# A retention-attention and two-MoE kernel: two column orders of the first MoE layer are interleaved

## The chip, the cores and the metric

The kernel runs on one core of one Trainium2 chip. The metric is the device time of one execution in microseconds (us). A core has a matrix engine (PE), a vector engine (DVE), a scalar engine (ACT), GpSimd (POOL) and a queue engine (SP) that issues transfers. Each works off its own list of instructions in a fixed order and waits for the others by semaphores. A kernel is timed over several executions; one more is recorded by the profiler, and all durations below are from that one.

## The reference

```python
# attention with decay: 2 batches, 8 heads, 768 tokens, head size 64, blocks of 64
out[:, :, sl] = (q k^T * Dmask) v + (q * lam_pow) kv_state     # kv_state runs over the blocks
# first MoE layer, dense: x is [1536, 512], w_in [512, 2048], w_out [2048, 512]
h = x @ w_in
g = h * np.clip(h + 3.0, 0.0, 6.0) / 6.0
x = g @ w_out
# second MoE layer: 8 experts, 192 tokens each
logits = x @ w_gate                      # every token goes to an expert with room, best logit first
out[mask] = np.maximum(x[mask] @ w1[e], 0.0) @ w2[e]
```

## The kernel before, in words

The 1536 tokens are 12 chunks of 128; chunks 0 to 5 are the first batch, 6 to 11 the second. Every matrix product that has to be exact is made from 16-bit pairs (a high and a low half), so one product is three matmuls (`mm3`, L221 to L223).

**Attention** of chunk c: scores S (L452), their masked copy sm on DVE (L458), the state product kv (L467) with its DVE step sbd, and the output xo (L494, L498). The two halves of xo leave through ACT (L504) and DVE (L505) as xT, the 16-bit pair that is the x of the first layer.

**The first layer** is 52 units of h, each one PSUM buffer of 512 columns for 12 matmul groups: group 0 is 8 units of chunks 0 to 3 one at a time (`h0_u`, the first four column blocks of w_in), group 1 is 12 units over chunks 0 to 3 together (`h1_u`, column blocks 4 to 15), group 2 is 8 units of chunks 4 and 5, group 3 is 8 units of chunks 6 and 7, group 4 is 16 units of chunks 8 to 11. A unit leaves by four instructions: r on ACT (L535) and DVE (L536), then the pair g by ACT (L406) and DVE (L416). h has three PSUM buffers.

**Weights.** w_in and w_out arrive as 64-bit numbers in eight parts each (`wis`, `wos`) and are turned into 16-bit pairs by a chain that changes engines: ACT L383 (L381 on DVE for the first three parts of w_in), POOL L385, then DVE L387, L389, L391, then ACT L406 and DVE L416. The part in work is called `wid` or `wod`. Each part of w_out is also transposed by DMA (`wt`, in the pool H of two buffers, which wid, wod and the logits' halves use too) and multiplied by the gate's weights (`wp`, L585 and L586), which gives the weights of the logits.

**Logits, routing, experts.** lq (L610) are the logits of four chunks each, lg (L625) sums them up. Then come seven routing phases (mp on PE, POOL L775, DVE L800 and L809, ACT L803), in which PE fills its time with x2p, the product g w_out (L647: 48 matmuls of 512 columns for each of chunks 0 to 7, of 384 columns for 8 to 11; their last 128 columns are x2q and x2t). After routing, rk and pos give each token its place, and POOL scatters the tokens by 24 indirect DMAs, 12 of `xsa` and 12 of `xsb` (L877). A transposing DMA brings each pair of experts its rows (`xs`, L897, L898), and the experts' products are hp (L922) and po (L952).

**What sets the order.** The program is not written in the order in which it runs. Each step is handed to a planner (`Plan`) with its engine, an estimated cost, what it depends on, its buffers and a key. The planner walks through an imagined time; of the steps that could start on an engine within a small window it takes the one with the smallest key. What comes out is one fixed list for each engine. A dependency that is given to the planner alone moves a step in these lists; at run time an instruction waits only for data, for a buffer, or for those ahead of it on its engine. `unit_key` is the key of each unit in a running count over the list `order`; `w0_key` is the key of the first part of w_out.

Of the kernel before, what the change touches and what calls it, by code (L numbers as in the profile page):

```python
# [16 lines left out]
NCH = 12  # L17
# [31 lines left out]
class Plan:  # L49
# [122 lines left out]
def c_se(n):  # L172
    return 0.1 + n * 0.00083
# [19 lines left out]
def fused_kernel(ctx, tc, raw_d, lam_d, win_d, wout_d, wg_d, w1_d, w2_d, out):  # L193
# [229 lines left out]

    RAW_KEY = [0, 0, 2, 2.5, 3.5, 6.5, 16, 17, 18, 19, 20, 21]

# [85 lines left out]
    h_mm = {}  # L511
    win = {}

    def h_unit(g, u, key, lo_eng):
# [11 lines left out]
        def mms():  # L526
            for f in range(nf):
# [6 lines left out]
        r = buf("Q", [P, nf, T], F32, f"r{g}_{u}")  # L534
        t = add("se", c_se(nf * T), lambda: se.activation(r[:], ps[:], AF.Relu, bias=c3, scale=2.0 ** -31), [t], [ps, r], key)  # L535
        t = add("ve", c_ve(nf * T), lambda: ve.scalar_tensor_tensor(r[:], r[:], 6.0 * 2.0 ** -11, ps[:], op0=OP.min, op1=OP.mult),  # L536
                [t], [ps, r], key)
        for c in cs:
            g_done.setdefault(c, []).extend(
                split(lambda: r[:], lambda: (gt[:, 0, fo:fo + nf, to:to + T], gt[:, 1, fo:fo + nf, to:to + T]), nf * T, 1.0, lo_eng, [t], [r, gt], key + 1)  # L540
                if c == c0 else g_done[c0][-1:])
# [9 lines left out]
    t = 20.0  # L551
    order = [(g, u) for g in range(5) for u in range(len(UNITS[g]))]
    for i, (g, u) in enumerate(order):
# [3 lines left out]
    for c in range(NCH):  # L557
        attention(c, max(0.5 + 4 * c, unit_key[GOF[c], 0] - 40) if c > 3 else 7 * c)
        if c == 0:
            weights(win_d, win, 1024.0, "wi", lambda k: 10 + 7 * k, lambda k: "ve",  # L560
                    lambda k: [0, 1, 3, 3, 6, 6, 7, 7][k], pre=win_ld)
    for g, u in order:
        h_unit(g, u, unit_key[g, u], "ve")

    warm_last.deps = [h_mm[order[10]]]

# [5 lines left out]
    t_pj = []  # L572
    w0_key = unit_key[4, 0] - 16

    def project(k, t, dst):
# [6 lines left out]
        def pj():  # L582
# [6 lines left out]
    weights(wout_d, wout, 2048.0, "wo", lambda k: w0_key + 7 * k, lambda k: "ve", lambda k: 30 + k, project,  # L589
            lambda k: [out_done[[4, 4, 6, 6, 8, 8, 10, 10][k]]])  # L590
    w1t = C([P, 16, NE], F32, "wpt")
# [450 lines left out]
```

## Time and profile before

| | |
|---|---|
| three timed runs | 512.02, 514.68, 515.46 us; median 514.68 |
| the profiled execution | 515.91 us; 514.0 us from its first to its last instruction |
| TensorE clock over the span | 0.986 of full speed |
| PE busy | 485.0 us, 94% |
| DVE busy | 397.8 us, 77% |
| ACT busy | 309.0 us, 60% |
| POOL busy | 166.6 us, 32% |

Busy shares are averages over stages with different limits. Up to about 50 us loads, conversions and the first attention chunks share the time; from 50 to 205 us runs the first layer with the rest of attention; from 215 to 345 us the routing phases; then scatter and the experts. A matmul's end is modelled, so a short wait on PE can be hidden in the row ahead of it; starts are the safer numbers.

### The profile page before, as it was taken

To read this page: it belongs to the slowest core of one execution; us is meant where nothing else is said; L and a number is where in the kernel's file an instruction comes from. 1 tells how busy PE (TensorE), PEld (TensorE's weight loads), DVE (VectorE), ACT (ScalarE), POOL (GpSimd) and SP (SyncE) were. 2 spreads that over 40 slices of the span, in tenths; PEclk is the share of its full clock that TensorE was granted. 3 is DMA by queue.
4 is the path that set the end of the run, shared out by engine and by line. 5 is a ranking of instruction groups with operands and counts; after the bars stand their busy time and mean duration, and the time that the engine had idled before them with its cause. 6 is when DMAs were issued, how large, how long until landed. Compare 5 with 4: busy or idle time off the path is not lost.

```text
span 514.0 us, 10307 instructions
## 1 busy us (share of the span) xinstructions
PE 485.0 (94%) x4241; PEld 296.7 (58%) x4243; DVE 397.8 (77%) x707; ACT 309.0 (60%) x486; POOL 166.6 (32%) x174
## 2 busy tenths in 40 slices
PE   7687998999999999999999999999969999999995
PEld 3476444688785444534434443556459676776762
DVE  7689999988688877589899889877524878889620
ACT  1476959764556664377669558745423767687510
POOL 2013343120222220167347436618860312223211
PEclk9889999999999999999999999999979999999999
DMA  7999326220264550000000000667368999995011
GB/s 224 400 416 412 148 83 246 84 42 2 83 246 91 97 94 8 2 1 1 1 1 2 1 1 7 240 246 240 132 149 261 327 400 356 360 354 215 1 42 41
DMA packets 44910, 77.86 MB, mean 151 GB/s; under 512 B 33080, under 2 KB 34112, under 8 KB 38720
## 3 DMA queue, kind: packets, MB, share of 16 engines
q1 hardware_dynamic: 42752, 70.82, 41.0%
q0 software_dynamic: 2112, 6.39, 3.3%
q8 instruction: 33, 0.54, 0.4%
q14 instruction: 13, 0.11, 0.1%
HBM read 63.46 MB, written 6.40 MB: 136 GB/s over the span
## 4 chain that ended last, share of the span: by engine, by line
DVE 38%; issue 22%; PE 18%; POOL 8%; ACT 8%; DMA 5%; POOLq 0%; SPq 0%; DVEq 0%; ACTq 0%
PE x2p L647 9%; DVE G L809 7%; DVE r L536 4%; DVE G L800 3%; DVE g L416 3%; POOL w L410 3%; POOL out L877 2%; ACT kd L439 2%; DVE sm L458 2%; ACT g L406 2%; DVE eq L782 2%; PE h L221 2%; DVE wid L391 2%; PE cp L828 2%; PE h L223 2%
## 5 line engine op out<-in xcount | busy, mean ns | idle before, releaser
L647 PE MATMUL x2p<-wo,g 128*128 128x512 f16 (+1 forms) x576 | 124.6, 362 | 0.0
L221 PE MATMUL h<-xT,wi 128*128 128x256 f16 (+2 forms) x304 | 90.8, 306 | 2.8 <-DVE r L536 2.8
L222 PE MATMUL h<-xT,wi 128*128 128x256 f16 (+2 forms) x304 | 90.7, 306 | 0.0
L223 PE MATMUL h<-xT,wi 128*128 128x256 f16 (+2 forms) x304 | 90.6, 306 | 0.0
L647 PEld LDWEIGHTS <-g 128*128 128x128 f16 x576 | 52.5, 99 | 55.6 <-issue 10.5
L775 POOL TENSOR_SCALAR eq<-mrow,m 128x128 bf16<-128x128 f32 x56 | 56.7, 1030 | 84.6 <-DVE on L748 52.1
L416 DVE SCALAR_TENSOR_TENSOR w<-ws,w 128x1024 f16<-128x1024 f32 x58 | 71.4, 1276 | 5.8 <-ACT w L406 5.8
L922 PE MATMUL hp<-xs,w 128*128 128x192 f16 x768 | 67.4, 251 | 3.8 <-DMA xs<-xsa 3.8
L922 PEld LDWEIGHTS <-w 128*128 128x128 f16 x768 | 65.1, 100 | 7.6 <-issue 5.2
L952 PE MATMUL po<-w,h 128*64 128x512 f16 (+1 forms) x384 | 64.1, 380 | 0.1
L406 ACT ACTIVATE w<-ws 128x1024 f16<-128x1024 f32 x64 | 63.9, 1048 | 0.1
L809 DVE TENSOR_SCALAR G<-mrow,m 128x1408 bf16<-128x1408 f32 (+10 forms) x77 | 52.0, 706 | 0.0
L385 POOL TENSOR_SCALAR wod<-wod 128x1024 f32<-128x1024 f32 x8 | 22.5, 2818 | 89.3 <-ACT wod L383 75.5
L406 ACT ACTIVATE g<-r 128x512 f16<-128x512 f32 (+1 forms) x52 | 30.8, 595 | 30.5 <-DVE r L536 29.6
L952 PEld LDWEIGHTS <-h 128*64 128x64 f16 (+1 forms) x384 | 29.0, 104 | 31.8 <-issue 1.7
L416 DVE SCALAR_TENSOR_TENSOR g<-r,g 128x512 f16<-128x512 f32 (+1 forms) x52 | 34.3, 662 | 11.4 <-ACT g L406 11.0
L536 DVE SCALAR_TENSOR_TENSOR r<-r,h 128x512 f32<-128x512 f32 (+1 forms) x52 | 33.1, 639 | 10.1 <-ACT r L535 9.8
L535 ACT ACTIVATE r<-h,c 128x512 f32<-128x512 f32 (+1 forms) x52 | 33.4, 644 | 10.9 <-PE h L223 10.8
L803 ACT ACTIVATE G<-mrow,m 128x1536 bf16<-128x1536 f32 (+3 forms) x28 | 39.4, 1407 | 0.8
L222 PEld LDWEIGHTS <-wi 128*128 128x128 f16 x304 | 30.6, 101 | 15.9 <-issue 3.2
L928 ACT ACTIVATE rr<-hp 128x384 f32<-128x384 f32 x32 | 15.6, 490 | 40.0 <-PE hp L922 39.8
L221 PEld LDWEIGHTS <-wi 128*128 128x128 f16 x304 | 30.5, 100 | 15.0 <-issue 1.5
(154 smaller groups left out, 693.2 us busy)
## 6 DMA issues: line engine op xcount, KB each, us to landing
ws<-w SPq DMA_DIRECT2D x32, 1024.0 KB, 9.3
raw<-raw SPq DMA_DIRECT2D x24, 512.0 KB, 10.0
wis<-w_in SPq DMA_DIRECT2D x8, 1024.0 KB, 14.1
wos<-w_out SPq DMA_DIRECT2D x8, 1024.0 KB, 7.8
tab<-tz SPq DMA_DIRECT2D x1, 512.0 KB, 6.3
wt<-wo SPq DMA_TRANSPOSE x16, 3.2
xsa<-xa,pos POOLq DMA_INDIRECT x12, 4.9
xsb<-xb,pos POOLq DMA_INDIRECT x12, 2.7
```

The lines of the kernel that those rows point to most:

```text
L221: te.matmul(ps, lh, rh, start=start, stop=False)
L222: te.matmul(ps, lh, rl, start=False, stop=False)
L223: te.matmul(ps, ll, rh, start=False, stop=stop)
L406: h = add("se", c_se(n), lambda: se.activation(dst()[0], src(), AF.Copy, scale=sc), deps, bufs, key, reserve)
L416: lo = add("ve", c_ve(n), lambda: ve.scalar_tensor_tensor(dst()[1], src(), sc, dst()[0], op0=OP.mult, op1=OP.subtract), [h], bufs, key)
L536: t = add("ve", c_ve(nf * T), lambda: ve.scalar_tensor_tensor(r[:], r[:], 6.0 * 2.0 ** -11, ps[:], op0=OP.min, op1=OP.mult), [t], [ps, r], ...
L647: te.matmul(ps[:], gsl(y, fc, j), w[:, z, fc % 4, d0:d1], start=(fc + y + z == 0), stop=(fc == 15 and y == 1))
L775: t_eq.append(add("ge", 1.06, lambda i=i, eq=eqs[0], mrow=mrow: ge.tensor_scalar(eq[:, i], mrow[:, P * i:P * i + P], m[:, i:i + 1], None, ...
L803: se.activation(G[:, z, 0:o], mrow[:, 0:o], AF.Sign, scale=-1.0, bias=m[:, i:i + 1])
L809: ve.tensor_scalar(G[:, z, o:], mrow[:, o:], m[:, i:i + 1], None, op0=OP.is_le)
L922: te.matmul(ps[:, i], w[:, z, kk % 2, cl], x[:, 2 * kk + y, CAP * i0:CAP * i0 + CAP], start=(i + kk + y + z == 0), stop=(i == 1 and kk == ...
L952: te.matmul(o, h1[e][:, y, k, cl], w2[e, fh][0][:, zz, f], start=(k + y + zz == 0), stop=(k == 7 and y == 1))
```

## The change

The list `order`, by which the units of h get their keys, is no longer group after group: the units of group 2 and, further on, of group 3 stand between pairs of group 1 from `h1_2` on. The keys of the loads of chunks 5 to 11, of w_in's parts from the third on and of w_out's parts are set to that order, the r and g steps get keys 45 and 20 below their unit's, and the loads of chunks 8 to 11 and of w_out get a dependency, for the planner, on a unit of h. The number of instructions of each kind stays.

```diff
--- before.py
+++ after.py
@@ -421,7 +421,7 @@
     xT, x_done, state_done, state_read = {}, {}, {}, {}
     out_done, kv_done = {}, {}
 
-    RAW_KEY = [0, 0, 2, 2.5, 3.5, 6.5, 16, 17, 18, 19, 20, 21]
+    RAW_KEY = [0, 0, 2, 2.5, 3.5, 4.5, 5.5, 6.5, 18, 19, 20, 21]
 
     def attention(c, key):
         s = c % 6
@@ -532,12 +532,12 @@
         t = add("pe", 12 * nf * c_pe(T), mms, w_done[f0 % 4 // 2:(f0 % 4 + nf - 1) // 2 + 1] + sum((x_done[c] for c in cs), []), [w, x, ps], key)
         h_mm[g, u] = t
         r = buf("Q", [P, nf, T], F32, f"r{g}_{u}")
-        t = add("se", c_se(nf * T), lambda: se.activation(r[:], ps[:], AF.Relu, bias=c3, scale=2.0 ** -31), [t], [ps, r], key)
+        t = add("se", c_se(nf * T), lambda: se.activation(r[:], ps[:], AF.Relu, bias=c3, scale=2.0 ** -31), [t], [ps, r], key - 45)
         t = add("ve", c_ve(nf * T), lambda: ve.scalar_tensor_tensor(r[:], r[:], 6.0 * 2.0 ** -11, ps[:], op0=OP.min, op1=OP.mult),
-                [t], [ps, r], key)
+                [t], [ps, r], key - 45)
         for c in cs:
             g_done.setdefault(c, []).extend(
-                split(lambda: r[:], lambda: (gt[:, 0, fo:fo + nf, to:to + T], gt[:, 1, fo:fo + nf, to:to + T]), nf * T, 1.0, lo_eng, [t], [r, gt], key + 1)
+                split(lambda: r[:], lambda: (gt[:, 0, fo:fo + nf, to:to + T], gt[:, 1, fo:fo + nf, to:to + T]), nf * T, 1.0, lo_eng, [t], [r, gt], key - 20)
                 if c == c0 else g_done[c0][-1:])
 
     def gsl(part, fc, j):
@@ -549,7 +549,12 @@
 
     unit_key = {}
     t = 20.0
-    order = [(g, u) for g in range(5) for u in range(len(UNITS[g]))]
+    order = [(0, u) for u in range(8)] + [(1, 0), (1, 1)]
+    for u in range(10):
+        order += [(2, v) for v in ((0, 1) if u == 0 else (u + 1,)) if v < 8]
+        order += [(1, 2 * u + 2), (1, 2 * u + 3)] if u < 5 else []
+        order += [(3, v) for v in ((0, 1) if u == 2 else (u - 1,)) if 1 < u < 9]
+    order += [(4, u) for u in range(16)]
     for i, (g, u) in enumerate(order):
         i -= 4
         unit_key[g, u] = t
@@ -557,12 +562,15 @@
     for c in range(NCH):
         attention(c, max(0.5 + 4 * c, unit_key[GOF[c], 0] - 40) if c > 3 else 7 * c)
         if c == 0:
-            weights(win_d, win, 1024.0, "wi", lambda k: 10 + 7 * k, lambda k: "ve",
-                    lambda k: [0, 1, 3, 3, 6, 6, 7, 7][k], pre=win_ld)
+            weights(win_d, win, 1024.0, "wi", lambda k: 10 + 7 * k if k < 2 else unit_key[1, 2 * k - 4] - 14, lambda k: "ve",
+                    lambda k: [0, 1, 3, 4, 5, 6, 7, 8][k], pre=win_ld)
     for g, u in order:
         h_unit(g, u, unit_key[g, u], "ve")
 
-    warm_last.deps = [h_mm[order[10]]]
+    warm_last.deps = [h_mm[order[8]]]
+    for c, n in zip(range(8, NCH), (19,21,23,25)):
+        for st in ld_raw[c]:
+            st.deps.append(h_mm[order[n]])
 
 
     t_wg = add("sp", 0.06, lambda: sy.dma_start(wg, wg_d), (), (), 40, 0, 1 << 14)
@@ -570,7 +578,7 @@
     wout = {}
     wpp = buf("pE", [P, 16, 2 * NE], F32, "wp")
     t_pj = []
-    w0_key = unit_key[4, 0] - 16
+    w0_key = unit_key[4, 0] - 70
 
     def project(k, t, dst):
         key = w0_key + 7 * k + 8
@@ -587,7 +595,7 @@
         t_pj.append(add("pe", 0.5, pj, tr + [t_wg, kv_done[10]], [wt, wpp], key))
 
     weights(wout_d, wout, 2048.0, "wo", lambda k: w0_key + 7 * k, lambda k: "ve", lambda k: 30 + k, project,
-            lambda k: [out_done[[4, 4, 6, 6, 8, 8, 10, 10][k]]])
+            lambda k: [h_mm[order[[18,20,22,24,26,28,30,32][k]]]])
     w1t = C([P, 16, NE], F32, "wpt")
 
     def wprime():
```

On DVE the place is the attention of chunks 4 and 5 (sm4 and sm5 are the masked scores, qd the scaled queries, r1 and g0_4 the exits of group 1's units, wid4 the fifth part of w_in, xT1 the exit of xo4). Before:

```order
L458 TENSOR_TENSOR sm4_0_926<-S4_0_831,tab_93 128x512
L458 TENSOR_TENSOR sm4_1_928<-S4_1_832,tab_93 128x512
L476 TENSOR_TENSOR sbd_85<-sbd_85,kv4_846 128x256
L443 TENSOR_TENSOR qd5_944<-raw5_431,tab_93 128x512
L536 SCALAR_TENSOR_TENSOR r1_3_897<-r1_3_897,h1_3_857 128x512
L458 TENSOR_TENSOR sm5_0_965<-S5_0_932,tab_93 128x512
L458 TENSOR_TENSOR sm5_1_968<-S5_1_933,tab_93 128x512
```

Now; sm4_1, qd5 and the L416 of wi1 stand directly ahead of these rows:

```order
L536 SCALAR_TENSOR_TENSOR r1_0_807<-r1_0_807,h1_0_775 128x512
L476 TENSOR_TENSOR sbd_85<-sbd_85,kv4_798 128x256
L408 TENSOR_SCALAR wgs_140<-wg_139 128x4x8
L416 SCALAR_TENSOR_TENSOR wgs_140<-wg_139,wgs_140 128x4x8
L387 TENSOR_SCALAR wid4_655<-wid4_655 128x1024
L416 SCALAR_TENSOR_TENSOR g0_4_833<-r1_0_807,g0_4_833 128x512
L443 TENSOR_TENSOR qd7_858<-raw7_650,tab_93 128x512
L389 SCALAR_TENSOR_TENSOR wid4_655<-wis4_214,wid4_655 128x1024
L505 SCALAR_TENSOR_TENSOR xT1_861<-xo4_0_810,xT1_861 128x2x128
L505 SCALAR_TENSOR_TENSOR xT1_861<-xo4_1_811,xT1_861 128x2x128
L458 TENSOR_TENSOR sm5_0_888<-S5_0_848,tab_93 128x512
L458 TENSOR_TENSOR sm5_1_890<-S5_1_849,tab_93 128x512
```

Between sm4_1 and sm5_1 stood four rows; now there are twelve, with two steps of w_in's conversion, the gate's weights wgs, and xT of chunk 4 among them.

On POOL the place is the scatter of the tokens. Before, from the eleventh scatter on (each has a MEMSET of one column ahead of it, and that is left out here):

```order
L877 DMA xsa_170<-xa_8_4152,pos_166 1536x768
...
L877 DMA xsb_171<-xb_2808,pos_166 1536x288
...
L877 DMA xsb_171<-xb_2808,pos_166 1536x288
...
L877 DMA xsb_171<-xb_2808,pos_166 1536x288
...
L877 DMA xsb_171<-xb_2808,pos_166 1536x288
...
L877 DMA xsa_170<-xa_8_4152,pos_166 1536x768
...
L877 DMA xsb_171<-xb_2808,pos_166 1536x288
```

Now, from the eleventh scatter on:

```order
L885 DMA xsb_171<-xb_2792,pos_166 1536x288
...
L885 DMA xsa_170<-xa_8_4163,pos_166 1536x768
...
L885 DMA xsb_171<-xb_2792,pos_166 1536x288
...
L885 DMA xsb_171<-xb_2792,pos_166 1536x288
...
L885 DMA xsb_171<-xb_2792,pos_166 1536x288
...
L885 DMA xsb_171<-xb_2792,pos_166 1536x288
...
L885 DMA xsb_171<-xb_2792,pos_166 1536x288
...
L885 DMA xsa_170<-xa_8_4163,pos_166 1536x768
...
L885 DMA xsb_171<-xb_2792,pos_166 1536x288
```

The last scatter of xsa was the sixteenth of 24 and is now the eighteenth; one more of xsb stands ahead of the last but one.

On SP the place is the loads of w_out (wos) among those of the late chunks (raw) and the transposes wt. Before:

```order
L257 DMA wos0_993<-w_out 128x2048
L257 DMA wos1_996<-w_out 128x2048
L249 DMA raw9_1049<-raw 128x1024 x2
L249 DMA raw10_1194<-raw 128x1024 x2
L257 DMA wos2_1224<-w_out 128x2048
L257 DMA wos3_1256<-w_out 128x2048
L249 DMA raw11_1299<-raw 128x1024 x2
L578 DMA_TRANSPOSE wt0_1337<-wo0_1304 128x8x128 x2
L257 DMA wos4_1816<-w_out 128x2048
L257 DMA wos5_1821<-w_out 128x2048
L257 DMA wos6_1951<-w_out 128x2048
L257 DMA wos7_1999<-w_out 128x2048
```

Now:

```order
L257 DMA wos0_1260<-w_out 128x2048
L249 DMA raw8_1292<-raw 128x1024 x2
L257 DMA wos1_1325<-w_out 128x2048
L249 DMA raw9_1362<-raw 128x1024 x2
L257 DMA wos2_1390<-w_out 128x2048
L249 DMA raw10_1417<-raw 128x1024 x2
L249 DMA raw11_1548<-raw 128x1024 x2
L586 DMA_TRANSPOSE wt0_1571<-wo0_1463 128x8x128 x2
L586 DMA_TRANSPOSE wt1_1671<-wo0_1463 128x8x128 x2
L586 DMA_TRANSPOSE wt2_1838<-wo1_1636 128x8x128 x2
L257 DMA wos3_1926<-w_out 128x2048
L257 DMA wos4_1928<-w_out 128x2048
```

The first four parts of w_out were loaded ahead of all transposes; now three are, and the other five stand behind the transposes of the first three, of which the third waits for a buffer of the pool H that PE's first wp has to read.

## Rows read from the trace of the kernel before

**Rows 1.** Waits of PE, 48 to 205 us: for whom, us in total, times, longest.

```profile
PE h L221 <- DVE r L536: 2.8, 3, 1.3
```

**Rows 2.** Timeline of PE, 40 to 100 us: start, us, line, tile, count, idle and releaser.

```profile
41.53 0.77 PE L494 MATMUL xo<-qd,sbd 64*64 64x128 f32 x8 [1.80 <-DVE xT L505]
...
50.16 0.38 PE L221 MATMUL h<-xT,wi 128*128 128x512 f16 x1 [0.81 <-DVE r L536]
...
58.24 1.16 PE L452 MATMUL S<-raw 64*128 64x128 f32 x16
59.33 0.69 PE L467 MATMUL kv<-raw,kd 128*64 128x64 f32 x16
...
70.57 0.45 PE L494 MATMUL xo<-qd,sbd 64*64 64x128 f32 x8
...
72.50 0.39 PE L221 MATMUL h<-xT,wi 128*128 128x512 f16 x1
```

**Rows 3.** Timeline of PE around the end of the first layer.

```profile
195.45 0.17 PE L585 MATMUL wp<-wgs,wt 128*128 128x16 f16 x1
...
195.85 0.38 PE L221 MATMUL h<-xT,wi 128*128 128x512 f16 x1
...
198.53 3.64 PE L610 MATMUL lq<-g,wps 128*32 128x512 f16 x64
202.10 0.39 PE L221 MATMUL h<-xT,wi 128*128 128x512 f16 x1
...
204.71 0.44 PE L625 MATMUL lg<-sel,ls 128*128 128x8 bf16 x12
...
214.67 1.47 PE L767 MATMUL mp<-ident,m 128*128 128x128 f32 x12
```

**Rows 4.** Timeline of DVE, 52 to 70 us.

```profile
56.27 1.94 DVE L391 SCALAR_TENSOR_TENSOR wid<-wis,wid 128x1024 int32<-128x1024 int32 x1
...
58.73 0.67 DVE L536 SCALAR_TENSOR_TENSOR r<-r,h 128x512 f32<-128x512 f32 x1
59.33 0.68 DVE L387 TENSOR_SCALAR wid<-wid 128x1024 int32<-128x1024 int32 x1
60.04 1.22 DVE L389 SCALAR_TENSOR_TENSOR wid<-wis,wid 128x1024 int32<-128x1024 int32 x1
61.19 1.22 DVE L416 SCALAR_TENSOR_TENSOR wi<-wid,wi 128x1024 f16<-128x1024 f32 x1
...
64.06 1.01 DVE L408 TENSOR_SCALAR wgs<-wg 128x32 f16<-128x32 f32 x1
```

**Rows 5.** Loads and conversions of w_out: ns min/median/max; DMA landing in us.

```profile
L385 POOL TENSOR_SCALAR wod<-wod x8: 2766/2766/3177, 85.5 to 180.7; 128x1024 f32<-128x1024 f32 x8
...
DMA to landing us min/median/max: 6.5/7.8/12.4
```

**Rows 6.** Timeline of POOL in the scatter.

```profile
346.56 1.92 POOL L877 DMA_INDIRECT xsa<-xa,pos  x1 [11.10 <-DVE pos L865]
...
368.86 1.97 POOL L877 DMA_INDIRECT xsa<-xa,pos  x1 [0.19 <-DVE w L416]
...
371.13 0.96 POOL L877 DMA_INDIRECT xsb<-xb,pos  x1 [0.19 <-issue]
...
372.40 0.96 POOL L877 DMA_INDIRECT xsb<-xb,pos  x1 [0.19 <-issue]
```

**Rows 7.** Timeline of PE in the scatter.

```profile
345.01 17.71 PE L647 MATMUL x2p<-wo,g 128*128 128x384 f16 x108
...
373.77 0.65 PE L691 MATMUL x2t<-ident,xq 128*128 128x128 f32 x4 [0.69 <-ACT xq L686]
378.26 4.00 PE L922 MATMUL hp<-xs,w 128*128 128x192 f16 x24 [3.84 <-DMA xs<-xsa]
```

**Rows 8.** Stretches: us, busy us (instructions) of each engine, TensorE clock, DMA share, GB/s.

```profile
40.00:50.00 10.00, 7.82 (x128) 6.88 (x129) 10.00 (x16) 5.63 (x12) 3.40 (x1) 1.00 1.03 412
...
378.00:382.00 4.00, 3.74 (x24) 3.44 (x24) 0.40 (x1) 0.00 (x0) 3.41 (x8) 0.50 0.65 162
```

## The prediction

> **What bounds the kernel now.** I read the table of stretches first, then the waits and the timeline of PE by start times, then DVE, then the scatter. From 50 to 205 us PE is the engine that sets the pace, and it is nearly full: the view of its waits names little more than 2.8 us for the h units, which wait for DVE's r to free a PSUM buffer [rows 1]. That is a lower bound, as a row's end is modelled. The upper bound comes from starts. The first stretch that the change touches begins where `h0_7` ends, at 50.16 - 0.81 = 49.35 [rows 2], and ends with `h4_15` at 204.71 [rows 3]: 155.4 us. The work in it: a unit of h takes 204.71 - 202.10 = 2.61, and there are 12 of group 1, 16 of groups 2 and 3 (the same columns, two times 256) and 16 of group 4, so 44 x 2.61 = 114.8; eight S of 59.33 - 58.24 = 1.09 are 8.7 and six kv of 0.69 are 4.1 [rows 2]; xo takes 72.50 - 70.57 = 1.93, eight of them less half of one (chunk 6 opens a batch and has no state to read) 14.5; eight wp of 195.85 - 195.45 = 0.40 are 3.2; lq0 and lq1 take 202.10 - 198.53 = 3.57 [rows 3]. Together 148.9. PE therefore loses 6.5 us to waits, and no reordering can win more than that there.
>
> From 205 to 345 the routing phases set the time, with x2p as PE's filling. After them the end hangs on POOL: 24 scatters without a break from 346.56 [rows 6], the last xsa at 368.86, the transposing DMA of xs, and hp at 378.26, before which PE stood idle for 3.84 us [rows 7]. From hp on PE is full to the end.
>
> **The change, part by part.** The lists of PE are the same up to `h0_7`, so nothing is won before it.
>
> *lq0 and lq1.* They stood ahead of `h4_15` and now stand behind it. `h4_15` ends 3.57 earlier. This carries through to the routing: between `h4_15` and the first mp stood one lq, three lg and 33 x2p, 214.67 - 204.71 = 9.96 [rows 3]; now stand three lq, three lg and 17 x2p. 16 x2p of 0.216 (a twelfth of 2.61) are 3.46, so the distance is 9.96 + 3.57 - 3.46 = 10.07. First mp: 3.5 earlier from this alone. The 16 x2p go into the phases and out behind them. Each phase holds 58 x2p as before, and what is left at the end is 33 of x2p9 where 12 were. That is 21 more at 17.71 / 108 = 0.164 [rows 7], 3.4 us, which fall into PE's time beside the scatter. There x2t ends at 374.42 and hp begins at 378.26, so they cost nothing as long as POOL is later.
>
> *The 6.5 us of old waits.* With groups 1, 2 and 3 interleaved and r keyed 45 earlier, r no longer stands behind long conversions when a PSUM buffer is due; I count all of them as gone, and put the new ones against them.
>
> *New waits, in order.* (1) xo3, ahead of 49.35: r and g of chunk 0 now stand ahead of xo2's exit on DVE. It waited 1.80 already [rows 2]; half of a 0.60 instruction more, 0.35. (2) xo4, 0.3. (3) S6. It needs the PSUM buffers that sm5 reads. Between the ends of sm4_1 and sm5_1 DVE now has qd5, r1_0, g0_4, qd7 and two sm at 0.60 (59.33 - 58.73), L387 at 0.71 (60.04 - 59.33), L389 and wi1's L416 at 1.15 (61.19 - 60.04) [rows 4], sbd and two halves of xT at 0.33 (half the columns, an estimate), and wgs, 0.2 if nothing disturbs it: 3.6 + 0.71 + 2.3 + 1.0 + 0.2 = 7.8. PE has xo4, S5 and `h1_1` meanwhile: 1.93 + 1.09 + 2.61 = 5.6. Wait: 2.2; with wgs at the 1.01 that it took beside a POOL instruction [rows 4], 3.0. I take 2.3. (4) xo6. Behind sm5_1, DVE has L391, r1_1, two sm6, g, wi2's L416, L387 and xT of xo5: 1.15 + 0.6 + 1.2 + 0.6 + 1.15 + 0.71 + 0.66 = 6.1, against S6, xo5, kv6 and S7 on PE, 1.09 + 1.93 + 0.69 + 1.09 = 4.8. Wait 1.2. (5) S9, S10 and xo9 together 0.9, one and a half instructions of 0.60. (6) The first four units of group 4, 0.5. (7) The conversions of w_out. Five parts now load behind the third wt, which waits for the first wp on PE. Counted back from the new end of `h4_15`, about 201.8: 16 units, the six wp among and ahead of them, `h3_5` to `h3_7`, xo11, `h2_7`, xo10 are 41.8 + 2.4 + 7.8 + 1.9 + 2.6 + 1.9 = 58.4, so near 143. wos3 lands 7.8 later [rows 5], near 151; five conversions then follow one another beside group 4, and each holds ACT's queue, with r of h behind it, for up to POOL's 2.77 [rows 5]. Three PSUM buffers cover 2 x 2.61 of that. Ends 0 and 2.77, once; I take the middle, 1.4, since no row shows these two beside each other. Sum of (1) to (7): 0.35 + 0.3 + 2.3 + 1.2 + 0.9 + 0.5 + 1.4 = 6.95; from both sides 3 (only S6, the surest, and two halves of an instruction) to 10.
>
> *PE's balance.* 3.5 + 6.5 - 6.95: `h4_15` and the first mp come about 3.0 earlier. The routing then runs as before, so POOL begins its scatter 3.0 earlier.
>
> *The scatter.* The last xsa was the 16th scatter and is now the 18th, behind two more xsb. An xsb takes 372.40 - 371.13 = 1.27 [rows 6], so 2 x 1.27 = 2.5; the other end is 372.40 - 368.86 = 3.5, the time at which the 18th scatter stood. I take 2.5, nearer to what a scatter of xsb costs. The data of that scatter comes from x2p11, which ended by 345.01 + 17.71 = 362.7 [rows 7], 6 us before its scatter; 3.4 us more of x2p, begun 3.0 earlier, leave that. xs, hp and the end come 3.0 - 2.5 = 0.5 earlier.
>
> *POOL beside DVE.* One L391 took 1.94 instead of about 1.15 while POOL ran L385 [rows 4], 0.8 more; this is within the middle that I took for (7). The Trainium skill (SBUF — State Buffer, "Who interferes with whom") says that a DVE instruction with two SBUF inputs and a POOL instruction that reads SBUF exclude each other for the whole instruction. The 1.94 does not bear that out, since it is far from 2.77 more; what full exclusion would make of the time is rival D.
>
> **The sum.** The profiled execution was 515.91, its span 514.0. 515.9 - 0.5 = 515.4. That execution is 1.2 above the median of the three, 514.68; in their terms 514.2.
>
> **Rivals.** *A: the interleaving does all it can.* Old waits go, none come: 3.5 + 6.5 = 10.0 on PE, less 2.5 in the scatter, -7.5, 507.2. For it: PE's old waits are all on DVE, and attention's DVE work is now spread. Against: DVE was busy 10.00 of 10.00 us at 40 to 50 [rows 8], it has no room to take xT, sm and conversions in earlier, and item (3) is read off its list. 0.15.
>
> *B: ACT is blocked by late loads of w_out (slower).* In ACT's list the L383 of wod3 and of wod4 stand ahead of r for `h3_5`. ACT then waits at them for a transfer, and three units later `h4_0` finds no PSUM buffer. `h4_0` is due at 201.8 - 41.8 - 2.4 = 157.6, so this decides if wos4 lands after about 155 (L383 of some 1.15 and r's two steps of 0.60 lie between). By the median wos3 lands near 151 and wos4 right behind it; by the longest, 12.4 [rows 5], both land 4.6 later and it is reached. Then the five conversions start late too, and the hold of 2.77 comes a second time: up to 4.6 + 2.8 = 7.4, 521.6. Chance 0.12.
>
> *C: the clock falls at S6.* After the idle 3.84 the granted clock was 0.50 from 378 to 382 [rows 7, 8], so at half speed, 1.2 of 2.4 GHz, 4 us of work took 4 for 2: price 2.0. After the 1.80 at 41.53 it stayed at 1.00 [rows 2, 8]. The forecast wait is 2.3, between the two. Then +1.5, 516.2. 0.14. The Trainium skill (TensorE: Matmul & The Clock Gate, "What's actually happening") has the same two levels, and a fall after idleness, which the rows show; by that page this wait could go either way.
>
> *D: DVE stands still beside POOL.* If L385 holds a DVE instruction of each of the five late parts for all of its 2.77, and not for the 0.8 of rows 4, DVE loses 5 x 2.0 = 10; three PSUM buffers cover 2 x 2.61 of it, so +4.8, 519.0. Against: the 1.94, which shows a stretch and no standstill, and L385 meets DVE in the lists before as well. Chance 0.04.
>
> The forecast itself, gains and losses of some microseconds that cancel, keeps 0.55.
>
> **How the numbers follow.** This kernel's measurement tells about 1%, 5.1 us, from no change. The forecast reaches from waits of 3 and 2.5 in the scatter (3.5 + 6.5 - 3 - 2.5 = -4.5, 510.2) to waits of 10 and 3.5 (+3.5, 518.2). With the nearer half of A and B the range is 508.5 to 519.5; what is left out is the far part of A and B. Faster by over 1% is the most of A with the edge of the forecast, 0.17; slower by over 1% is the most of B with part of D, 0.13; the rest 0.70.
>
> **What would show it.** `h4_15` ending near 201.5; S6 starting 2 us late behind sm5; idle before h units near the wod instructions; first mp 10 us behind `h4_15`; the last xsa scatter 24.8 us after the first, where it was 368.86 - 346.56 = 22.3 [rows 6]; hp near 377.8. It would be wrong if DVE's list is paced otherwise than I counted, if routing takes the moved x2p badly, or if hp starts with the clock at another level.

## The result: 1.4% slower, and the profile after

The changed kernel takes 522.64 us, median of four runs (519.76 to 522.87), against 514.64 for the kernel before in the same series: a ratio of 1.0143 [1.011, 1.0175]. The forecast was 514.2, with a range that ended at 519.5. The profiled execution took 522.58, its span is 520.9 (before 515.91 and 514.0).

The quickest way into such a result is a table of milestones, so that each microsecond gets a place. "Rk" is the start of the ranking that stands ahead of the scatter; all times are from the span's start.

| milestone | before | after | later by | gained or lost since the row above |
|---|---|---|---|---|
| `h0_7` starts | 47.85 | 49.21 | 1.36 | +1.36 |
| `h4_0` starts | 156.54 | 159.88 | 3.34 | +1.98 |
| `h4_15` ends | 204.71 | 208.95 | 4.24 | +0.90 |
| first mp | 214.67 | 218.99 | 4.32 | +0.08 |
| rk | 344.63 | 349.33 | 4.70 | +0.38 |
| last xsa scatter | 368.86 | 376.97 | 8.11 | +3.41 |
| hp starts | 378.26 | 385.81 | 7.55 | -0.56 |
| end of the span | 514.0 | 520.9 | 6.9 | -0.65 |

The rows of `h4_0` and `h4_15` need a second look. Two of the eight wp, 0.80 us, moved from behind the start of `h4_0` to ahead of it: they are part of the +1.98. And lq0 and lq1, 3.57 us, no longer stand ahead of `h4_15` either, so +0.90 there hides a loss of 0.90 + 3.57 + 0.80 = 5.3.

**PE's waits after the change**, 48 to 215 us (for whom, releaser, us in total, times, longest), in the place of [rows 1]:

```profile
PE S L452 <- DVE sm L458: 3.2, 2, 1.7
PE h L221 <- DVE r L536: 2.5, 1, 2.5
PE wp L594 <- DMA wt<-wo: 1.3, 2, 0.8
PE xo L498 <- DVE xT L505: 1.0, 1, 1.0
```

The wait of h for r, three times before, has come down to one, but that one is 2.5 us. S and xo waited for attention's own steps on DVE before as well, though for less; before, in the same view as [rows 1]:

```profile
PE xo L498 <- DVE sm L458: 0.8, 2, 0.7
PE S L452 <- DVE sm L458: 0.2, 1, 0.2
```

Now S and xo L498 wait 3.2 and 1.0 us. These are new waits, of which the forecast had some and missed others.

**PE by start times** (start, us, line, tile, count, idle before and releaser), in the place of [rows 3] and [rows 7]:

```profile
62.90 1.75 PE L452 MATMUL S<-raw 64*128 64x128 f32 x16 [1.67 <-DVE sm L458]
...
134.13 1.16 PE L452 MATMUL S<-raw 64*128 64x128 f32 x14 [1.51 <-DVE sm L458]
...
180.93 0.38 PE L221 MATMUL h<-xT,wi 128*128 128x512 f16 x1 [2.45 <-DVE r L536]
...
208.95 5.53 PE L618 MATMUL lq<-g,wps 128*32 128x512 f16 x96
...
218.99 1.47 PE L775 MATMUL mp<-ident,m 128*128 128x128 f32 x12
...
385.81 17.66 PE L930 MATMUL hp<-xs,w 128*128 128x192 f16 x192 [3.27 <-DMA xs<-xsa]
```

S6 waits at 62.90, S9 at 134.13, and at 180.93 `h4_7` finds no PSUM buffer. From the end of `h4_15` to the first mp are 10.04 us. At 385.81 hp still waits for the scatter, 3.27 us.

**DVE ahead of that wait** at 180.93, in the manner of [rows 4]:

```profile
175.22 1.23 DVE L416 SCALAR_TENSOR_TENSOR wo<-wod,wo 128x1024 f16<-128x1024 f32 x1
176.36 0.69 DVE L387 TENSOR_SCALAR wod<-wod 128x1024 int32<-128x1024 int32 x1
177.08 1.23 DVE L389 SCALAR_TENSOR_TENSOR wod<-wos,wod 128x1024 int32<-128x1024 int32 x1
178.34 1.94 DVE L391 SCALAR_TENSOR_TENSOR wod<-wos,wod 128x1024 int32<-128x1024 int32 x1
180.20 1.27 DVE L536 SCALAR_TENSOR_TENSOR r<-r,h 128x512 f32<-128x512 f32 x2
```

ACT had done its half of `r4_4` at 175.61 + 0.67. DVE's half, which frees the PSUM buffer, is at 180.20, behind four conversion steps of w_out, 1.23 + 0.69 + 1.23 + 1.94. A row's length overlaps the next row a little; starts tell more.

**How full DVE is.** In the table of stretches (us, then busy us and instructions of PE, PE's weight loads, DVE, ACT and POOL, PE's clock, DMA share, GB/s) the 30 us from 158 to 188, which hold the first half of group 4, read before and after:

```profile
158.00:188.00 30.00, 29.95 (x224) 14.79 (x223) 24.14 (x32) 18.51 (x28) 8.30 (x3) 1.00 0.50 89
```

```profile
158.00:188.00 30.00, 27.41 (x128) 12.77 (x127) 29.76 (x34) 19.00 (x28) 11.53 (x4) 0.94 0.24 69
```

DVE went from 24.14 of 30 to 29.76 of 30, and PE from 29.95 down to 27.41. The reason stands in POOL's list, whose L385 is one step of each conversion. Before, and after:

```profile
169.67 2.77 POOL L385 TENSOR_SCALAR wod<-wod 128x1024 f32<-128x1024 f32 x1 [8.31 <-ACT wod L383]
180.73 2.77 POOL L385 TENSOR_SCALAR wod<-wod 128x1024 f32<-128x1024 f32 x1 [8.30 <-ACT wod L383]
```

```profile
153.94 5.50 POOL L385 TENSOR_SCALAR wod<-wod 128x1024 f32<-128x1024 f32 x2 [31.13 <-ACT wod L383]
164.87 3.08 POOL L385 TENSOR_SCALAR wod<-wod 128x1024 f32<-128x1024 f32 x1 [5.43 <-ACT wod L383]
170.94 3.80 POOL L385 TENSOR_SCALAR wod<-wod 128x1024 f32<-128x1024 f32 x1 [2.99 <-ACT wod L383]
177.72 3.21 POOL L385 TENSOR_SCALAR wod<-wod 128x1024 f32<-128x1024 f32 x1 [2.98 <-ACT wod L383]
```

Before, the conversions came 11.1 us apart. Now POOL had none for 31 us, and then five came within 24 us, the last two 6.1 and 6.8 us behind the one before them.

**The clock behind the wait:**

```profile
182.00:184.00 2.00, 2.00 (x7) 0.77 (x6) 2.00 (x4) 0.98 (x2) 0.00 (x0) 0.55 0.09 19
184.00:186.00 2.00, 2.00 (x7) 0.73 (x6) 1.93 (x3) 0.98 (x2) 0.00 (x0) 0.59 0.96 120
186.00:190.00 4.00, 4.00 (x21) 1.81 (x19) 2.49 (x4) 2.24 (x4) 0.00 (x0) 1.00 0.34 66
```

After an idle 2.45 us the granted clock was 0.55 and 0.59, near the lower of its two levels, 1.2 GHz, for 4 us. `h4_7` and `h4_8` took 1.26 and 0.42 longer than the 2.61 of a unit.

**POOL in the scatter**, in the place of [rows 6]:

```profile
351.26 1.92 POOL L885 DMA_INDIRECT xsa<-xa,pos  x1 [12.05 <-DVE pos L873]
...
372.74 1.66 POOL L885 DMA_INDIRECT xsb<-xb,pos  x1 [0.19 <-issue]
374.70 1.97 POOL L885 DMA_INDIRECT xsb<-xb,pos  x1 [0.19 <-issue]
376.97 1.97 POOL L885 DMA_INDIRECT xsa<-xa,pos  x1 [0.19 <-DVE w L416]
```

The last xsa comes 25.7 us after the first, where it was 22.3. The two xsb right ahead of it took 1.66 and 1.97, not the 0.96 of [rows 6].

### The profile page after: what moved, and what is told of

Its sections match the earlier page's. It is cut to its first block, busy times and chain, and to the rows that moved or that the text cites. A ratio compares the mean times of both kernels' runs of the same rounds, so it can differ in the third digit from the quotient of the medians.

```text
span 520.9 us, 10310 instructions
## 1 busy us (share of the span) xinstructions
PE 488.5 (94%) x4241; PEld 299.0 (57%) x4243; DVE 400.5 (77%) x707; ACT 309.6 (59%) x486; POOL 171.2 (33%) x174
## 3 DMA queue, kind: packets, MB, share of 16 engines
q1 hardware_dynamic: 42752, 70.82, 41.5%
## 4 chain that ended last, share of the span: by engine, by line
PE 37%; DVE 31%; issue 12%; ACT 6%; DMA 6%; POOL 5%; SPq 2%; POOLq 0%; DVEq 0%; ACTq 0%
PE hp L930 9%; PE po L960 7%; DVE G L817 7%; PE x2p L655 6%; DVE G L808 3%; PE h L221 3%; PE h L222 3%; PE h L223 3%; DVE r L536 2%; ACT kd L439 2%; POOL xsa L885 2%; DVE g L416 2%; DMA xsa<-xa,pos 2%; DVE eq L790 2%; DMA raw<-raw 2%
## 5 line engine op out<-in xcount | busy, mean ns | idle before, releaser
L416 DVE SCALAR_TENSOR_TENSOR w<-ws,w 128x1024 f16<-128x1024 f32 x58 | 71.3, 1276 | 13.1 <-ACT w L406 13.1
L385 POOL TENSOR_SCALAR wod<-wod 128x1024 f32<-128x1024 f32 x8 | 27.2, 3408 | 72.8 <-ACT wod L383 72.8
L416 DVE SCALAR_TENSOR_TENSOR g<-r,g 128x512 f16<-128x512 f32 (+1 forms) x52 | 35.4, 693 | 8.6 <-ACT g L406 8.5
L222 PEld LDWEIGHTS <-wi 128*128 128x128 f16 x304 | 30.5, 100 | 16.9 <-issue 3.7
L221 PEld LDWEIGHTS <-wi 128*128 128x128 f16 x304 | 30.4, 100 | 15.7 <-issue 1.9
L223 PEld LDWEIGHTS <-wi 128*128 128x128 f16 x304 | 30.5, 100 | 15.1 <-issue 0.8
```

The source lines that it names most:

```text
L221: te.matmul(ps, lh, rh, start=start, stop=False)
L222: te.matmul(ps, lh, rl, start=False, stop=False)
L223: te.matmul(ps, ll, rh, start=False, stop=stop)
L416: lo = add("ve", c_ve(n), lambda: ve.scalar_tensor_tensor(dst()[1], src(), sc, dst()[0], op0=OP.mult, op1=OP.subtract), [h], bufs, key)
```

## Experiments

The total of two executions of the same kernel differs by up to 6 us here, in part for a cause that lies ahead of the change (last section). So verdicts below come from stretches inside a run, and totals only where several runs stand behind them. The kernel before took 514.43, 515.36 and 513.33 in the three series of runs (15, 19 and 1 of them).

**1. Leave the conversions of the late parts of w_out out of DVE.** Parts 3 to 7 are loaded, and ACT and POOL do their steps, but DVE's L387, L389 and L391 are not issued for them, so these parts of w_out are left unconverted. (`by_cols` is false for w_out, so the condition holds for its parts from k = 3 on.)

```diff
-            a = add("ve", 0.7, lambda b=b: ve.tensor_scalar(
+            a = add("ve", 0.7, lambda k_=k, b=b: None if by_cols < (k_ >= 3) else ve.tensor_scalar(
...
-            a = add("ve", 1.23, lambda b=b, st=st: ve.scalar_tensor_tensor(
+            a = add("ve", 1.23, lambda k_=k, b=b, st=st: None if by_cols < (k_ >= 3) else ve.scalar_tensor_tensor(
...
-            a = add("ve", 1.23, lambda b=b, hi=hi: ve.scalar_tensor_tensor(
+            a = add("ve", 1.23, lambda k_=k, b=b, hi=hi: None if by_cols < (k_ >= 3) else ve.scalar_tensor_tensor(
```

> The changed kernel with the three DVE steps of w_out's conversion (L387, L389, L391) left out for parts 3 to 7; ACT's and POOL's steps, all loads and all lists otherwise the same. Theory 1 (five conversions of 4.3 us of DVE each, crowded beside group 4, put r of h late, and the 2.45 us wait before h4_7 then drops the clock): the wait before h4_7 and the stretch at half clock are gone, h4_0 to the end of h4_15 takes 44 to 45 us where it took 49.1, the whole about 518. Theory 2 (ACT's queue is held by loads of w_out that land late, rival B): ACT still waits at L383, the wait before h4_7 stays at 2 us or more, the whole 521 to 523.

From the start of `h4_0` to the end of `h4_15` it took 206.13 - 161.55 = 44.58, against 49.07 in the changed kernel. PE's waits from 150 to 205 us are now this row alone, and none of them is for h:

```profile
PE wp L594 <- DMA wt<-wo: 1.5, 2, 0.9
```

The loads, ACT's steps and POOL's L385 were all still there, at the same places of the lists, and ACT still waited for the loads at two L383, 2.01 and 0.82 us (1.52 and 0.81 in the changed kernel). So the 4.5 us come with DVE's steps, and not from ACT's blocking at a late load, nor from POOL's work by itself. One run took 520.05, more than these 4.5 would leave, because in it the clock fell at S6, where it had stayed up in the changed kernel, after the same idle 1.67 us:

```profile
62.50 2.67 PE L452 MATMUL S<-raw 64*128 64x128 f32 x16 [1.67 <-DVE sm L458]
```

and in the table of stretches:

```profile
64.00:66.00 2.00, 2.00 (x21) 1.45 (x20) 1.98 (x4) 1.57 (x2) 0.00 (x0) 0.50 0.38 90
```

From S6 to xo6 it took 8.66 where the changed kernel took 6.79: 1.9 us.

**2. Fill the idle time ahead of `h4_7`.** Eight matmuls into a PSUM buffer that nothing reads follow `h4_6`; nothing waits less for DVE, but PE has work where it stood idle.

```diff
-        ps = buf("pA", [P, nf, T], F32, f"h{g}_{u}")
+        ps = buf("pA", [P, nf, T], F32, f"h{g}_{u}"); dm = [buf("pC", [P, 512], F32, "dm")] if (g, u) == (4, 6) else []
...
+            for _ in range(8 if (g, u) == (4, 6) else 0): te.matmul(dm[0][:], w[:, 0, 0, 0:P], x[:, 0, 0], start=True, stop=True)
```

> The changed kernel with eight matmuls of 512 columns more (1.7 us) behind h4_6, into a PSUM buffer that nobody reads, in the time in which PE waits for h4_7's buffer. If the idle wait is what drops the clock: granted clock 1.00 from 182 to 186, h4_7 takes 2.6 where it took 3.85, the end 1.5 to 1.8 earlier, about 521. If the clock falls for another reason: h4_7 unchanged at 3.8, the whole 522 to 524.

The wait before `h4_7` is 0.72, and the clock stays:

```profile
182.00:184.00 2.00, 2.00 (x11) 0.88 (x9) 1.97 (x4) 1.27 (x3) 0.00 (x0) 1.00 0.51 98
184.00:186.00 2.00, 2.00 (x11) 0.94 (x10) 1.97 (x2) 0.62 (x2) 0.00 (x0) 1.00 0.86 164
```

`h4_7` takes 2.59. From the start of `h4_0` (159.15) to the end of `h4_15` (206.44) it took 47.29, 1.8 less than the 49.07 of the changed kernel: the fall of the clock had cost 1.26 + 0.42 = 1.7. Median 519.06 of six runs, ratio to before 1.0084 [1.0056, 1.0113].

**3. The changed kernel with the last xsa in 16th place again.** The xsb from the fifth on wait in the planner for the last xsa.

```diff
-                [t_pos] + t_xb[j] + ids_in, [xbb], GK + NCH + j, 0, 2 * P * XB) for j in range(NCH)]
+                [t_pos] + t_xb[j] + ids_in, [xbb], GK + NCH + j, 0, 2 * P * XB) for j in range(NCH)]; [st.deps.append(t_sa[11]) for st in t_sb[4:]]
```

> The changed kernel with the last scatter of xsa in the 16th place again, as before the change, all other lists the same. Theory 1 (POOL's order sets the start of hp): the last xsa starts 22.3 to 23.5 us after the first where it was 25.7, hp starts 2.2 to 3.3 us earlier, the whole 519.3 to 520.4. Theory 2 (the 21 more x2p behind routing, 3.4 us of PE, now set it): the last xsa or hp is later than its place allows, gain under 1 us, the whole above 521.6.

POOL's first and last xsa, then PE at the start of hp:

```profile
347.65 1.92 POOL L885 DMA_INDIRECT xsa<-xa,pos  x1 [12.05 <-DVE pos L873]
...
369.16 1.63 POOL L885 DMA_INDIRECT xsa<-xa,pos  x1 [0.19 <-issue]
```

```profile
378.27 0.66 PE L699 MATMUL x2t<-ident,xq 128*128 128x128 f32 x4 [0.69 <-ACT xq L694]
378.76 16.19 PE L930 MATMUL hp<-xs,w 128*128 128x192 f16 x192
```

The last xsa is 21.5 behind the first, and hp follows x2t without a wait: from here PE's own x2q and x2t set the time. From rk to hp it took 33.04 (36.48 in the changed kernel), from hp to the end 133.6 (135.1), since without the wait there is no fall of the clock at hp. That is 4.9 us. The median of ten runs is 515.38 (513.65 to 518.88), ratio 1.0042 [1.0011, 1.0072]: 7.3 under the changed kernel's, of which the scatter explains 4.9; what remains is of the size by which the runs differ among themselves.

**4. The kernel before with the last xsa in 14th place.** The same edit on the kernel before, with `t_sb[2:]`.

> The kernel before with the last scatter of xsa in the 14th place instead of the 16th. Theory 1 (hp waits for that scatter): hp starts about 3.5 us earlier, near 374.8, when x2t ends; the whole 511, or 509 if the clock does not fall at hp any more. Theory 2 (xsb, whose last scatter stays at 381, becomes what the experts wait for): PE waits for xs from xsb inside hp and the gain is under 1.5 us, 513 or more.

PE by start times, and a stretch around the start of hp:

```profile
371.40 0.66 PE L691 MATMUL x2t<-ident,xq 128*128 128x128 f32 x4 [0.69 <-ACT xq L686]
371.89 12.04 PE L922 MATMUL hp<-xs,w 128*128 128x192 f16 x144
```

```profile
372.00:376.00 4.00, 4.00 (x51) 4.00 (x49) 2.96 (x3) 1.72 (x3) 3.62 (x5) 1.00 0.39 114
```

The first scatter is at 344.19 and the last xsa at 362.74, 18.6 behind it. hp starts 27.7 behind the first scatter, where it was 31.7 [rows 6, 7]: 4.0 won. It keeps a clock of 1.00, where before it was 0.50 after the idle 3.84 [rows 8]; from hp to the end it took 133.8, not 135.7: 1.9 won. Median 508.71 of four runs (507.6 to 509.01), ratio **0.9896 [0.9858, 0.9935]**. This version beats both kernels, by one line of the planner's conditions.

**5. The kernel before with lq0 and lq1 behind `h4_15`.** This does one part of the change alone.

```diff
-            deps += g_done[j]
+            deps += g_done[j] + [h_mm[4, 15]]
```

> The kernel before with lq0 and lq1 behind h4_15; the lists up to there are those of before, those behind it come out as in the changed kernel (17 x2p before the first mp, 33 x2p9 left after routing, last xsa in the 18th place). Theory 1 (a gain of 3.5 us ahead of routing that the planner's scatter order gives back): first mp 9.9 to 10.1 us behind the end of h4_15 and 3.5 us earlier, last xsa 25 to 26 us after the first where it was 22.3, the whole 514 to 515, no change. Theory 2 (the time ahead of routing is what counts): 511.

PE by start times:

```profile
200.71 5.47 PE L610 MATMUL lq<-g,wps 128*32 128x512 f16 x96
...
210.69 1.47 PE L767 MATMUL mp<-ident,m 128*128 128x128 f32 x12
...
376.08 1.12 PE L691 MATMUL x2t<-ident,xq 128*128 128x128 f32 x4 [3.40 <-ACT xq L686]
378.01 17.85 PE L922 MATMUL hp<-xs,w 128*128 128x192 f16 x192 [0.81 <-DMA xs<-xsa]
```

`h4_15` ends 200.71 - 156.06 = 44.65 behind the start of `h4_0`, before 48.17: the 3.5 that the forecast named are there, and the first mp comes 9.98 behind `h4_15`. At the first scatter 3.95 us are won. Yet hp comes at 378.01, where it was 378.26. The planner's lists behind the routing come out as in the changed kernel: 33 x2p of the last units are left, the last xsa is in 18th place, and it finds its data late:

```profile
342.61 1.92 POOL L877 DMA_INDIRECT xsa<-xa,pos  x1 [10.99 <-DVE pos L865]
...
369.79 0.96 POOL L877 DMA_INDIRECT xsa<-xa,pos  x1 [3.33 <-DVE xa L662]
```

27.2 us behind the first, for 22.3 before. Median 513.88 of ten runs, ratio 0.9966 [0.9936, 0.9996]. So the edit on lq alone is enough to move the last xsa, and the first layer's gain is given back behind the routing. Not all of that is the place in the list: ACT's exit of the last x2p came only at 368.43, 6.4 us after PE had gone on to x2q (in the changed kernel 0.2 us after), and x2t too waited for ACT, 3.40 us. Why that exit came late was not found.

**6. Both edits on the kernel before.**

> The kernel before with lq0 and lq1 behind h4_15 and the last xsa in the 14th place. Theory 1 (with the scatter out of the way PE is full from routing to the end, and the x2p that lq displaced cost there what lq won): within 1 us of the 508.7 of the scatter edit alone; hp starts right behind x2t. Theory 2 (the lq gain carries through once POOL is out of the way): 505.

PE at the start of hp:

```profile
372.94 0.66 PE L691 MATMUL x2t<-ident,xq 128*128 128x128 f32 x4 [0.69 <-ACT xq L686]
373.44 12.04 PE L922 MATMUL hp<-xs,w 128*128 128x192 f16 x144
```

Median 509.65 of six runs, ratio 0.9899 [0.9861, 0.9937]: no better than experiment 4 alone. With hp no longer waiting for POOL, x2t ends the stretch, and that depends on PE's whole work ahead of it. From the first mp to hp it took 163.0 us, in experiment 4 159.6: the 3.5 us that lq had won come back as 3.4 us of x2p behind the routing. lq0 and lq1 moved, but they did not become shorter; what PE did not do before the routing it now does behind it.

**7. The changed kernel with sm of chunks 8 to 11 earlier in DVE's list.** S9 waited at 134.13 for sm steps whose input, S8, had been there since 118.7 but which DVE did at 130.46 and 133.39.

```diff
-                            [t_ss, dec_in], [pss[i], sm, tabb], key))
+                            [t_ss, dec_in], [pss[i], sm, tabb], key - (40 if c > 7 else 0)))
```

> The changed kernel with the key of the masked scores sm of chunks 8 to 11 lowered by 40, so that DVE takes sm8 to sm11 ahead of the exits r and g of h, as they come; ACT, POOL and SP nearly the same lists. Theory 1 (sm8 was ready at 118.7 and stood until 133.4 behind exits whose keys the change lowered): the waits at S9, S10 and xo9, 3.3 us together, fall under 1 us, and from the start of S8 to the start of h4_0 it takes 38.5 to 40 us where it took 42.6; the whole about 519.5. Theory 2 (DVE is full there whatever the order): 42 us or more, the whole 522 to 523.

PE's list changes with it: S9 stands at 120.06, ahead of units of h that it followed, but the work from S8 to `h4_0` is the same. That stretch took 41.28, for 42.59 in the changed kernel. The waits ahead of S9, S10 and xo9 are gone from PE's waits at 110 to 160:

```profile
PE wp L594 <- DMA wt<-wo: 0.6, 1, 0.6
PE kv L467 <- issue: 0.2, 1, 0.2
```

But only 1.3 of the 3.2 us that stood at these three came back: S9, S10 and S11 now took 1.67, 1.60 and 1.39 for the 1.09 of an S. So the order cost part of it; what the rest is, this run does not show (experiment 9 tells more). Median 519.13 of six runs, 1.0075 [1.0048, 1.0103]. The 2.5 us ahead of an h unit of group 4 stayed, and the clock fell there and at S6.

**8. The changed kernel with w_out loaded and keyed as before.**

```diff
-    w0_key = unit_key[4, 0] - 70
+    w0_key = unit_key[4, 0] - 16
...
-            lambda k: [h_mm[order[[18,20,22,24,26,28,30,32][k]]]])
+            lambda k: [out_done[[4, 4, 6, 6, 8, 8, 10, 10][k]]])
```

> The changed kernel with the key and the planner's dependencies of w_out's parts as they were before the change (the planner then also moves wp and lq behind h4_15 and puts all 12 xsa first). Theory 1 (the new w_out order is what costs beside group 4): no wait of over 1 us in group 4, h4_0 to the end of h4_15 in 44 to 46 us; but the logits come later, the first mp more than 14 us behind h4_15. Theory 2 (the interleaving is what costs): waits of 5 us from h4_0 to h4_15 stay.

Group 4 runs without any wait of PE from 150 to 205 us, 199.83 - 157.59 = 42.24. The conversions are spread again, and so they end late: lq starts at 214.24, and the first mp is 24.3 behind `h4_15`:

```profile
214.24 5.37 PE L618 MATMUL lq<-g,wps 128*32 128x512 f16 x96
...
224.12 1.15 PE L775 MATMUL mp<-ident,m 128*128 128x128 f32 x9
```

One run, 525.05. The last wp stands at 212.02, behind the last conversion, which DVE ended at 201.5, and its transposing DMA; DVE itself then stood idle for 9.10 us. So crowded, the conversions stop PE beside group 4; spread and late, they hold up lq by the length of their chain, and not by a full DVE.

**9. No conversions of w_out on DVE at all, in the changed kernel; 10. the same in the kernel before.** The three DVE steps of experiment 1 are left out for all eight parts (`k_ >= 0`). The second tells what the interleaving does when conversions are out of the way.

> The changed kernel with L387, L389 and L391 left out for all eight parts of w_out, all lists otherwise the same. Theory 1 (the first three conversions, now between 106 and 131 us, fill DVE and make S9, S10 and xo9 wait): from the start of S8 to the start of h4_0 it takes 38.5 to 40 us where it took 42.6. Theory 2 (sm8 to sm11 and xT stand behind exits of h in DVE's list, whatever else is there): 41.5 us or more. Either way no wait from h4_0 to h4_14.

> The kernel before with the same three steps left out for all eight parts, as a control. If the conversions cost the old order little, as they are spread from 85 to 190 us: from the end of h0_7 to the start of h4_0 it takes 105.5 to 107 us where it took 107.3, and the whole moves by less than 2 us. If DVE was already full of them: 104 or less.

| stretch | before | before, none | after | after, none |
|---|---|---|---|---|
| end of `h0_7` to `h4_0` | 107.3 | 106.0 | 109.2 | 107.4 |
| `h0_7` starts to first mp | 166.8 | 165.4 | 169.8 | 163.6 |

Without the conversions the whole time is 513.56 for the changed kernel and 513.36 for the kernel before. The changed kernel then reaches the first mp 1.8 earlier than the kernel before, but lq is worth 3.5 there; so the rest of the change loses 1.7 by itself. It loses 0.6 of it in the interleaved stretch (107.4 - 106.0, less two wp of 0.40 that moved in) and 1.1 beside group 4, where a wp waited 1.1 for its transposed weights. PE's waits of the changed kernel without conversions hold the row

```profile
PE wp L594 <- DMA wt<-wo: 1.7, 2, 1.1
```

With its conversions, the kernel before loses 1.4, the changed kernel 6.2, of which 1.7 is the fall of the clock: the same DVE work costs four times as much. From S8 to `h4_0` the changed kernel without conversions took 40.71, between the two expectations: S9 no longer waited, and S10 and xo9 lost 1.2 as before.

Only w_out's conversions are left out here; w_in's stay. So in the kernel before without them, h waits for r exactly as in [rows 1], and the waits of xo for sm are gone:

```profile
PE h L221 <- DVE r L536: 2.8, 3, 1.3
```

## Why the prediction was wrong

The forecast, in the profiled execution's terms, put the end 0.5 earlier; it came 6.9 later. The 7.4 us lie here:

| term | forecast | measured | miss |
|---|---|---|---|
| ahead of the end of `h0_7` | +0.35 | +1.36 | 1.0 |
| waits from there to `h4_0` | 4.7 | 7.6 | 2.9 |
| waits from `h4_0` to the end of `h4_15` | 1.9 | 5.3 | 3.4 |
| `h4_15` to first mp | 10.07 | 10.04 | 0 |
| routing | 0 | +0.4 | 0.4 |
| rk to hp | +2.5 | +2.85 | 0.35 |
| hp to the end | 0 | -0.65 | -0.65 |

The waits are counted as the forecast counted its 6.5: the stretch by starts, less the work in it. From the end of `h0_7` to `h4_0` that is 109.2 - 101.6 (three wp stand there, where one did), and from `h4_0` on 49.07 - 16 x 2.61 - 5 x 0.40.

**lq0 and lq1: right.** 3.5 won before the routing and 10.0 to the first mp, in the changed kernel and, alone, in experiment 5. What the forecast did not see is that this move alone is enough to send the last xsa to the back (experiment 5). That part of the change was worth 0.3% alone and nothing once the scatter was out of the way, by experiments 5 and 6.

**The 6.5 of old waits "all gone": right for the places, wrong as a gain.** With the kernel before counted in the same way, all 6.5 lay between `h0_7` and `h4_0` (107.3 - 100.8). By starts 3.0 of it stood at the three h units that waited for r; the rest stood mainly at S and xo, for sm and xT. So the reason given, r behind long conversions, covers half, and there it held: PE's waits in the changed kernel show no unit of h in that stretch. But the waits did not leave PE, they moved from h to S, xo, kv and wp. Without w_out's conversions 5.2 are left in the kernel before (106.0 - 100.8) and 5.8 in the changed kernel (107.4 - 101.6), so the interleaving alone won nothing here.

**S6 and xo6: right in size, S6 in part by luck.** 2.3 and 1.2 were forecast; by starts it was 1.83 ahead of S6 and 0.59 between its halves, 2.4, and 1.0 ahead of xo6. For S6 two misses cancel: from sm4_1 to sm5_1 DVE took 8.6 and not 7.8, since the g at 58.32 took 1.52 beside POOL's L385, and PE had kv4, 0.62, to do as well. (Thirteen rows stand between sm4_1 and sm5_1, not the twelve named above; the sum had them all.)

**S9, S10 and xo9: wrong in size**, 0.9 for "one and a half instructions" of 0.60. S9 lost 1.99, S10 0.89 and xo9 0.31, together 3.2; kv4 lost 0.5, more than the 0.3 put down for xo4 there, and one wp lost 0.73, for which the forecast had nothing. For S6 the forecast added up DVE's list; for S9 and S10 it did not, and there the sm steps stood 12 us late in it. In part of that time DVE stood idle, 1.82 us, and waited for POOL:

```profile
122.84 0.69 DVE L387 TENSOR_SCALAR wod<-wod 128x1024 int32<-128x1024 int32 x1 [1.82 <-POOL wod L385]
```

Experiment 7 won 1.3 of the 3.2 by moving the sm steps, experiment 9 won 1.9 by leaving out the conversions.

**The conversions beside group 4: the step that failed most.** They were costed as one hold of POOL's 2.77, halved: 1.4, with 0.5 for the first units. The measured 5.3 is mainly the 2.6 ahead of `h4_7`, then 1.26 + 0.42 at the low clock, and 0.93 of wp. With the DVE steps left out 4.5 of it goes (experiment 1), with the loads and POOL's steps still there. The forecast priced the conversion's longest step against three PSUM buffers, and did not add up the engine: the late conversions 6 to 7 us apart, each 0.85 + 1.22 + 1.56 + 1.23 = 4.9 of DVE by its mean rows, with the exits of two and a half units of h, about 0.68 each and some of their g. That is a DVE busy 29.76 of 30 us. Before, at 11.1 us apart, it was busy 24.14. That the lack of slack is the cause, and not the place of r behind four conversion steps, is argued from these sums: a run with r ahead of them in DVE's list was not made.

**The scatter: right mechanism, short in size.** The last xsa went from 16th to 18th place and came 3.4 later behind the first, not 2.5; the other end that I gave was 3.5. The two xsb right ahead of it took 1.66 and 1.97 and not the 0.96 of [rows 6], which was read at a place where DVE did nothing beside them (last section). hp made up 0.6 of that, so 2.85 on the path. Experiments 3 and 4 show that this was a cost that could be taken away, and that it was there in the kernel before as well.

**The rivals.** A, the interleaving winning all it can, is refuted by experiments 9 and 10. (The times of A and C are worked out from the measured 514.7, those of B and D from the forecast 514.2.) B came near in time, 521.6, with another mechanism: the loads did land near 152.7, but leaving them late and taking DVE's steps out ends the wait (experiment 1), so ACT's block wasn't it. C was right that a wait of this size can drop the clock, and wrong about where: not at S6 in the changed kernel's profile, but ahead of `h4_7`. Experiment 2 prices it at 1.8. By the Trainium skill (TensorE: Matmul & The Clock Gate, "What's actually happening") idleness lowers the clock; the runs agree with that, in the rows at 182 to 186. D, DVE standing still beside POOL, is refuted: beside the late L385, L391 took 1.56 on average and L389 1.22, nowhere near 2.77 more. It was POOL's step that stretched: to 3.80 at 170.94, where an L389 of 1.23 had begun 0.05 earlier, and once, at 117.39, to 5.42, while DVE went through L389, a g and L391 in 2.9. With DVE's three steps left out that same L385 took 2.77 (at 114.24 in experiment 9). The Trainium skill (SBUF — State Buffer, "SBUF: two separate sides") says that of a DVE instruction with two SBUF inputs and a POOL instruction that reads SBUF the one that starts first gets the shared ports for its whole length, and the other stands still. The rows agree where DVE started first. Where POOL did they do not: an L389 at 70.82 took its usual 1.20 inside an L385 of 2.77.

What stays open: the 0.4 in the routing was not followed further. The 1.0 ahead of `h0_7` is of the size by which runs of one list differ (last section).

## What to carry to other kernels

Before packing an engine's helper work into a shorter stretch, add up that engine's busy time there: at 24 of 30 us no unit of group 4 waited, at 29.8 of 30 one waited 2.5 us and the clock fell behind it. It is a warning and not a rule: in the kernel before DVE was busy 9.97 of the 10 us from 90 to 100, and PE had no wait there. A gain counts only if the last releaser behind it moves as well: here 3.5 us in the first layer vanished at a scatter whose order the planner had changed as a side effect, while putting that one scatter two places ahead, with nothing gained before it, won 1%. And price the new waits with the same care as the first: the two that were summed off the list came true within half a microsecond, one of them in part by luck, and the ones rounded to "an instruction or so" or halved between two ends were off by a factor of about three.

## What the runs showed that was not expected

- **Equal waits, unequal clocks.** S6 stood idle for 1.67 or 1.68 in the changed kernel and in experiments 1, 2, 3, 7 and 9. The granted clock fell behind it in 1 and 7 (0.50) and in none of the others. The wait of about 2.5 in group 4 dropped it in all three profiles that had it (after, experiments 3 and 7); the 0.72 of experiment 2 did not.
- **The start differs from run to run of the same lists.** In experiment 3's profile the clock was 1.00 all through 20 to 36 us, and `h0_7` came 3.3 us earlier than in the changed kernel's, with the same lists up to there; the kernel before had 0.50 at 22 to 24 and 32 to 34 us. Ten runs of that kernel lie between 513.65 and 518.88. So of the changed kernel's +1.36 at `h0_7`, 0.8 is already there at the first xT of chunk 0, 21.00 for 20.16; in experiment 2, with the changed kernel's lists up to there, it was 19.92.
- **Some scatters take twice the time: those beside a step of DVE.** In the kernel before and in experiment 4, whose lists agree up to the 13th, the 4th, 15th and 16th took 1.96 to 1.97 where most take 0.96; in the changed kernel and in experiment 3 it was the 6th (1.97) and the 16th to 19th (1.63 to 1.97). So a price read off one place of the list did not hold for the next list. The traces tell what these places share. In the twelve profiles here 71 scatters (without the first of each) took more than 1.05, and all 71 began while DVE had an L416 of the experts' weights w under way; of the other 205, 7 did. In the changed kernel seven such L416 ran without a break from 372.34 to 380.37, beside the last xsa and the two xsb ahead of it. No run moved them away, so the cause is read from the traces and not shown by an edit.
